# Output rounds of a two-product kernel: spread evenly over the steps and started three steps earlier, with another start and tail

## The chip, the cores and the metric

The kernel runs on one core of a Trainium2 chip. The metric is the device time of one execution in microseconds (us). The granted clock is the share of TensorE's full clock that the profile lists; half clock is 0.5. Ratios are the mean time of one kernel's runs over that of the other's runs of the same rounds on the same chip, so they are not quite the ratio of the medians that stand beside them.

## The reference, cut to what matters

```python
# a 7-tap causal convolution along the sequence, taps by softmax, one set per head
w = softmax(weight)                                   # 8 heads x 7 taps
att = einsum('hk,bskhg->bshg', w, windows(x))         # 8 x 4096 x 192
# then two products with ELU between
h = att.reshape(32768, 192) @ w_in                    # 192 x 2048
g = where(h > 0, h, exp(min(h, 0)) - 1)
out = g @ w_out                                       # 2048 x 192, float32
```

## The kernel before

The tokens go through in 32 tiles of 1024, each in 16 steps of 128 hidden columns. I write h(n) for the first product of step n. Steps are counted from 0, over the whole run (h(16) opens tile 1) or, in the listings, within a tile (h(4) is the one of its step 4). ACT is ScalarE, POOL GpSimd and DVE VectorE; PSUM is the memory that TensorE writes its products to, and SBUF the memory that holds the operands. One step is this chain over four engines:

```python
# TensorE: h(n), six matmuls into slot k of three PSUM slots (two banks each)
wait_slot(k)                 # the step (or convolution) that had this slot is through with it
for j in range(3):
    for r in range(2):       # two row tiles of 64, one bank each
        matmul(H[:, k % 3, GS*r : GS*(r+1)], w_in[...], att[...], start=(j == 0), ...)
# ACT, then POOL, then DVE, two halves of 512 columns each
E  = exp(H)                                  # ACT
E  = max(min(E, 1), 0)                       # POOL
gT = max(E - 1, H)                           # DVE; frees the slot
```

The second product is made of output rounds. A round is two matmuls, one per row tile of 64, into the two banks of the accumulator `ops`. A half (256 of 512 token rows in each of two groups) takes 64 rounds: every piece of gT is used with row tile 0 into bank 0 and row tile 1 into bank 1, and once more with the banks exchanged. Two row tiles may not add into one bank at the same time, so TensorE waits at an exchange for the run of rounds before it. The Trainium skill (PSUM — Partial Sum Buffer, "PSUM bank collisions raise a hardware error") has it that different row tiles cannot access one bank at once and that software must order them.

```python
LAG = -1                                     # first output round of tile t: step 16(t+1)-1
HALF_STEPS = (10, 10, 6, 6, 10, 11, 11)      # rounds in 7 of 8 steps; none in the eighth
CONV_AT = ((4, 1, 1), (12, 2, 0))            # a convolution in steps 4 and 12 of a tile
...
            mid = (r0 + r1) // 2 if convs else r1
            order.append(("o", t, half, r0, mid))
            for k, g in convs:
                conv_at(k, g)                # in the middle of its step's rounds
            if mid < r1:
                order.append(("o", t, half, mid, r1))
...
                    for r in range(r0, r1):
                        second, (q, kb) = r // (NR // 2), divmod(r % (NR // 2), 2)
                        W(s_tt, 2 * (NQ * t + q) + 2)            # gT is there
                        if second:
                            W(s_swap, 2 * (2 * t + half + 1))    # one exchange a half
```

A convolution takes one of the three PSUM slots as well, and ACT copies it out (1.02 us). At the end of each half ACT copies the accumulator out (`osb`, 0.82 us); the first round of the next half waits for that copy.

## Time and profile before

| | before |
|---|---|
| time, median (before the change was run) | 756.66 us |
| span of the profiled run | 754.1 us |
| eight steps (half a tile) with a convolution | 11.32 us |
| first product of tile 1 starts (step 16) | 38.3 us |
| start of the last first product to the end | 16.6 us |

The page's busy times, with the share of the span and the number of instructions of each engine (PEld is TensorE's weight load):

```profile
PE 739.3 (98%) x13860; PEld 512.0 (68%) x13860; DVE 635.7 (84%) x1041; ACT 646.8 (86%) x1163; POOL 660.2 (88%) x1104
```

The groups of instructions with most time (line, engine, what is written and read; busy time, mean ns of one; idle time ahead of them and who ended it):

```profile
L500 DVE SCALAR_TENSOR_TENSOR gT<-E,H 128x512 f16<-128x512 f32 x1024 | 630.5, 681 | 98.7 <-POOL E L354 90.4
L437 ACT ACTIVATE E<-H 128x512 f32<-128x512 f32 x1024 | 546.2, 605 | 86.9 <-PE H L646 73.4
L676 PE MATMUL ops<-w_out,gT 64*128 64x192 f16 x8064 | 414.6, 243 | 0.9 <-DVE gT L500 0.9
L646 PE MATMUL H<-att,w_in 64*128 64x512 bf16 x3072 | 409.5, 379 | 5.7 <-DMA w_in<-w_in 3.4
```

TensorE hardly waits for anybody; DVE, ACT and POOL have 99, 87 and 79 us of idle time ahead of these instructions (POOL's line is not shown). The mean times of one matmul (243 and 379 ns) are from its start to its modelled end and overlap, so the pace is read from starts. Here is the order of time of TensorE over the steps around a convolution (start, us to the modelled end of the last one, what, how many):

```profile
404.78 0.66 PE L676 MATMUL ops<-w_out,gT 64*128 64x192 f16 x12
405.32 0.82 PE L646 MATMUL H<-att,w_in 64*128 64x512 bf16 x6
405.98 0.99 PE L676 MATMUL ops<-w_out,gT 64*128 64x192 f16 x20
406.80 0.81 PE L646 MATMUL H<-att,w_in 64*128 64x512 bf16 x6
407.45 0.57 PE L676 MATMUL ops<-w_out,gT 64*128 64x192 f16 x10
407.96 0.66 PE L619 MATMUL H<-Tr,xg 128*24 128x24 bf16 x40
408.55 0.67 PE L676 MATMUL ops<-w_out,gT 64*128 64x192 f16 x12
409.06 0.81 PE L646 MATMUL H<-att,w_in 64*128 64x512 bf16 x6
409.70 1.07 PE L676 MATMUL ops<-w_out,gT 64*128 64x192 f16 x22
410.61 1.46 PE L646 MATMUL H<-att,w_in 64*128 64x512 bf16 x12
```

From 405.32 to 405.98 six matmuls of a first product are issued (0.65 us); from 405.98 to 406.80 ten rounds (0.082 us each). Everything stands shoulder to shoulder. The step with the convolution is the one that starts at 406.80, which I call h(4). From h(4) to h(6) at 410.61 are 3.81 us. The last line holds two first products at once (x12): the step without rounds. ACT in the same stretch:

```profile
407.66 1.09 ACT L437 ACTIVATE E<-H 128x512 f32<-128x512 f32 x2 [0.39 <-PE H L646]
408.67 1.02 ACT L417 ACTIVATE csb<-H 128x1024 bf16<-128x1024 f32 x1
409.91 1.09 ACT L437 ACTIVATE E<-H 128x512 f32<-128x512 f32 x2 [0.21 <-PE H L646]
410.88 0.82 ACT L408 ACTIVATE osb<-ops 128x768 f32<-128x768 f32 x1
411.57 0.62 ACT L437 ACTIVATE E<-H 128x512 f32<-128x512 f32 x1
```

The matmuls of h(6) end at 411.42 or so (410.61 + 0.81); its Exp starts at 411.57, 0.11 us later than ACT could, because of the copy-out of the accumulator. In square brackets stands the idle time of the engine and who ended it.

Last, the stretches of the run by windows (us of each engine's busy time, granted clock, DMA share, GB/s): to h(16), to h(32), to the last first product, to the end.

```profile
12.00:38.30 26.30, 19.08 (x218) 7.51 (x216) 18.96 (x31) 18.97 (x37) 18.29 (x31) 0.87 0.71 128
38.30:61.70 23.40, 23.33 (x472) 16.38 (x474) 18.90 (x31) 20.21 (x36) 19.27 (x33) 1.00 0.40 86
61.70:737.50 675.80, 675.80 (x12820) 472.07 (x12816) 589.27 (x958) 599.29 (x1075) 611.70 (x1023) 1.00 0.43 95
737.50:754.10 16.60, 11.98 (x264) 10.58 (x260) 4.33 (x7) 3.73 (x7) 2.90 (x5) 1.00 0.24 73
```

In the 675.8 us of the third line TensorE is busy for 675.8. The first line holds the only slow clock (mean 0.87): at the start TensorE waited 3.4 us for a part of w_in that is copied inside SBUF, and ran at half clock from 16.9 to 23.7 us.

### The profile page before, as it was taken

What the parts mean: (1) busy time and instruction counts of PE and PEld (TensorE: products, weight loads), DVE (VectorE), ACT (ScalarE), POOL (GpSimd) and SP (SyncE); (2) the same over time, 40 slices, a digit from 0 to 9 for tenths busy, and PEclk for the clock granted to TensorE, in tenths of its full rate; (3) what the DMA queues carried; (4) which work ended last, traced back from release to release, by engine and by line L of the source; (5) the groups of instructions that cost most, each with busy time, mean ns of one, the idle gap of its engine ahead of it and who ended that gap; (6) DMA issues with size and microseconds to landing.
All of it is one profiled execution on the core that took longest, in us unless ns stands there. A gap on an engine that the chain in (4) does not pass through costs nothing.

```text
span 754.1 us, 32225 instructions
## 1 busy us (share of the span) xinstructions
PE 739.3 (98%) x13860; PEld 512.0 (68%) x13860; DVE 635.7 (84%) x1041; ACT 646.8 (86%) x1163; POOL 660.2 (88%) x1104
## 2 busy tenths in 40 slices
PE   6899999999999999999999999999999999999997
PEld 3367667767767767767767767767767767767676
DVE  3888898888888888888888888888888888888893
ACT  3888888888888888888888888889889889889882
POOL 5888998998998998998998998998998998998882
PEclk9899999999999999999999999999999999999999
DMA  9434345354355354355354355354355354355112
GB/s 176 101 87 93 93 105 112 77 107 92 92 108 110 76 109 91 93 108 110 75 111 92 89 110 109 74 112 92 88 112 109 72 114 90 87 115 107 58 44 64
DMA packets 106590, 72.79 MB, mean 97 GB/s; under 512 B 44488, under 2 KB 105808, under 8 KB 106448
## 3 DMA queue, kind: packets, MB, share of 16 engines
q1 hardware_dynamic: 66432, 54.77, 24.1%
q0 software_dynamic: 39600, 15.39, 19.1%
q8 instruction: 108, 1.77, 1.0%
q10 hardware_dynamic: 416, 0.59, 0.3%
q14 instruction: 34, 0.28, 0.1%
HBM read 44.00 MB, written 41.42 MB: 113 GB/s over the span
## 4 chain that ended last, share of the span: by engine, by line
PE 94%; DMA 2%; ACT 1%; DVE 1%; issue 0%; POOL 0%; SPq 0%
PE H L646 45%; PE ops L676 44%; PE H L619 5%; DMA w_in<-w_in 1%; DMA w_in<-in_moe_w_in_dram 1%; PE H L676 1%; ACT E L437 1%; DVE gT L500 1%; DMA att<-conv_slots 0%; DMA conv_slots<-csb 0%; ACT csb L417 0%; PE ops L537 0%; POOL w_in L312 0%; POOL E L354 0%; SPq L279 0%
## 5 line engine op out<-in xcount | busy, mean ns | idle before, releaser
L500 DVE SCALAR_TENSOR_TENSOR gT<-E,H 128x512 f16<-128x512 f32 x1024 | 630.5, 681 | 98.7 <-POOL E L354 90.4
L354 POOL TENSOR_SCALAR E<-E 128x512 f32<-128x512 f32 x1024 | 605.5, 615 | 78.7 <-ACT E L437 76.3
L437 ACT ACTIVATE E<-H 128x512 f32<-128x512 f32 x1024 | 546.2, 605 | 86.9 <-PE H L646 73.4
L676 PEld LDWEIGHTS ops<-w_out,gT 64*128 64x128 f16 x8064 | 342.2, 94 | 109.7 <-ACT osb L408 10.8
L676 PE MATMUL ops<-w_out,gT 64*128 64x192 f16 x8064 | 414.6, 243 | 0.9 <-DVE gT L500 0.9
L646 PE MATMUL H<-att,w_in 64*128 64x512 bf16 x3072 | 409.5, 379 | 5.7 <-DMA w_in<-w_in 3.4
L646 PEld LDWEIGHTS H<-att,w_in 64*128 64x128 bf16 x3072 | 130.5, 94 | 107.6 <-DVE gT L500 4.2
L417 ACT ACTIVATE csb<-H 128x1024 bf16<-128x1024 f32 x60 | 61.4, 1024 | 0.0
L408 ACT ACTIVATE osb<-ops 128x768 f32<-128x768 f32 x63 | 51.5, 817 | 5.1 <-PE ops L676 5.1
L307 POOL DMA_DIRECT2D xg<-in_x_dram x62 | 52.2, 842 | 0.4 <-issue 0.4
L619 PE MATMUL H<-Tr,xg 128*24 128x122 bf16 (+1 forms) x2400 | 39.3, 209 | 0.0
L619 PEld LDWEIGHTS H<-Tr,xg 128*24 128x24 bf16 x2400 | 30.1, 92 | 9.5 <-issue 9.5
L511 DVE COPY osb<-H 128x384 f32<-128x384 f32 x1 | 0.6, 558 | 8.9 <-PE H L676 8.9
L537 PE MATMUL ops<-zw 64*128 64x512 bf16 x20 | 4.6, 455 | 1.6 <-ACT csb L417 1.6
L532 PE MATMUL ops<-zw 128*128 128x512 bf16 x11 | 4.9, 632 | 1.3 <-DVE zw L450 1.3
L676 PE MATMUL H<-w_out,gT 64*128 64x192 f16 x128 | 5.6, 243 | 0.1
L676 PEld LDWEIGHTS H<-w_out,gT 64*128 64x128 f16 x128 | 5.2, 94 | 0.3 <-PE H L676 0.3
L400 ACT ACTIVATE osb<-H 128x384 f32<-128x384 f32 x1 | 0.5, 491 | 4.7 <-PE H L676 4.7
L532 PEld LDWEIGHTS ops<-zw 128*128 128x128 bf16 x11 | 1.5, 144 | 3.7 <-issue 2.5
L537 PEld LDWEIGHTS ops<-zw 64*128 64x128 bf16 x20 | 1.2, 110 | 4.0 <-ACT csb L417 2.6
L375 ACT ACTIVATE xT<-H 64x24 bf16<-64x24 f32 x1 | 0.2, 188 | 3.4 <-PE H L556 3.4
L312 POOL DMA_DIRECT2D w_in<-in_moe_w_in_dram x4 | 2.7, 680 | 0.3 <-DMA wh<-in_weight_dram 0.3
(46 smaller groups left out, 27.8 us busy)
## 6 DMA issues: line engine op xcount, KB each, us to landing
out_dram<-osb SPq DMA_DIRECT2D x127, 192.0 KB, 2.7
conv_slots<-csb SPq DMA_DIRECT2D x62, 256.0 KB, 2.5
att<-conv_slots SPq DMA_DIRECT2D x186, 64.0 KB
xg<-in_x_dram POOLq DMA_DIRECT2D x31, 240.0 KB, 5.0
xg<-in_x_dram POOLq DMA_DIRECT2D x31, 192.0 KB, 4.4
w_out<-in_moe_w_out_dram POOLq DMA_DIRECT2D x1, 768.0 KB, 16.2
xf<-in_x_dram ACTq DMA_DIRECT2D x1, 384.0 KB, 3.1
xf<-in_x_dram SPq DMA_DIRECT2D x1, 384.0 KB, 3.7
```

The source lines that it names most:

```text
L307: g.dma_start(xg[:, b, w0:w1, :], src).then_inc(s_x[b][part - 1], 16)
L312: g.dma_start(w_in[HP * r : HP * (r + 1), :, c0:c1], moe_w_in.rearrange("(p j) f -> p j f", j=3)[:, :, c0:c1],).then_inc(s_w[k], 16)
L354: g.tensor_scalar(out=E[:, n % NE, u, :], in0=E[:, n % NE, u, :], scalar1=1.0, scalar2=0.0, op0=ALU.min, op1=ALU.max,).then_inc(s_clp)
L408: a.activation(osb[:, b, :, :, :].rearrange("p g k d -> p g (k d)"), ops[:, :, 0 : 2 * D], ACT.Copy,).then_inc(s_oev)
L417: return a.activation(csb[:, m % 4, b0:b1, :], conv_bank(m)[:, b0:b1, :], ACT.Copy)
L437: a.activation(E[:, n % NE, u, :], H[:, k, GS * u : GS * (u + 1)], ACT.Exp).then_inc(s_exp)
L500: v.scalar_tensor_tensor(out=gT[:, s % NG3, q, u, :], in0=E[:, n % NE, u, :], scalar=1.0, in1=H[:, slot_of_pair[n] % 3, GS * u : GS * (u + ...
L532: pe.matmul(ops[:, 0, :], zw[:, 0:P], zw[:], start=True, stop=True)
L537: pe.matmul(ops[:, r, :], zw[HP * r : HP * (r + 1), 0:P], zw[HP * r : HP * (r + 1), :], start=True, stop=True, tile_position=(HP * r, 0),)
L619: ins = pe.matmul(to[SLOT * q : SLOT * q + CPH, hb, o : o + nc_], xg[:, s % NXB, w, CPH * h : CPH * (h + 1)], Tr[:, h, CW - c0 - nc_ : CW ...
L646: ins = pe.matmul(H[:, k % 3, GS * r : GS * (r + 1)], w_in[HP * r : HP * (r + 1), j, FC * q : FC * (q + 1)], att[HP * r : HP * (r + 1), s ...
L676: ins = pe.matmul(acc[:, g, D * kb : D * (kb + 1)], gT[HP * rt : HP * (rt + 1), t % NG3, q, g, t0 : t0 + P], w_out[HP * rt : HP * (rt + 1) ...
```

## The change

The change has four parts: output rounds start at step 12 of their tile instead of step 15, so that fewer are left for the tail; each step has eight rounds, and row tiles and banks are exchanged at each step, so that a round needs only the gT pieces that are already there; the rounds of the tail are interleaved so that they need not wait for an exchange; and the start loads w_in in four chunks, three of them straight to both halves of SBUF, and casts x first. The core of the diff:

```diff
-LAG = -1
-WCOLS = ((0, 256), (256, 1024), (1024, 2048))
-Q_PART = (0,) * 2 + (1,) * 6 + (2,) * 8
-WARM = (11, 1)
-HALF_STEPS = (10, 10, 6, 6, 10, 11, 11)
+LAG = -4
+QB = 4
+WCOLS = ((0, 256), (256, 640), (640, 1280), (1280, 2048))
+Q_PART = (0,) * 2 + (1,) * 3 + (2,) * 5 + (3,) * 6
+WARM = (9, 1)
...
+            for i in range(2 * NQ // QB):
+                n = NQ * (t + 1) + LAG + 8 * half + i
+                q0 = QB * (i // 2)
+                rounds_at[n] = [
+                    (t, half, q, kb, i % 2) for q in range(q0, q0 + QB) for kb in range(2)
+                ]
...
+    tail = (
+        piece(0, 0, 8, 14, (0, 1)) + piece(1, 0, 0, 12, (0,))
+        + piece(0, 1, 8, 14, (0, 1)) + piece(1, 1, 0, 12, (0,))
+        + piece(1, 0, 0, NQ, (1,))
+        + piece(0, 1, 14, NQ, (0, 1)) + piece(1, 1, 12, NQ, (0,))
+        + piece(0, 0, 14, NQ, (0, 1)) + piece(1, 0, 12, NQ, (0,))
+        + piece(1, 1, 0, NQ, (1,))
+    )
...
+        slot_of_pair[n] = take_slot(("h", n))
+        order.append(("h", n))
+        if n in EARLY_CONV:
+            conv_at(*EARLY_CONV[n])
         if s:
-            convs += [(s + ahead, g) for at, ahead, g in CONV_AT if at == i and n < NP]
+            for at, ahead, g in CONV_AT:
+                if at == i and s + ahead < NS:
+                    conv_at(s + ahead, g)
         if n in rounds_at:
-            mid = (r0 + r1) // 2 if convs else r1
-            order.append(("o", t, half, r0, mid))
-            for k, g in convs:
-                conv_at(k, g)
-            if mid < r1:
-                order.append(("o", t, half, mid, r1))
+            order.append(("o", rounds_at[n]))
...
             load_w_in(0, (0, 1))
-            load_w_in(1, (0,))
-            for part in (1, 2):
-                load_x(1, part)
-            load_w_in(2, (0,))
+            load_w_in(1, (0, 1))
+            load_x(1, 1)
+            load_w_in(2, (0, 1))
+            load_x(1, 2)
+            load_w_in(3, (0,))
```

The convolution now stands right behind h(4), ahead of all rounds of its step. And a half now ends in the step before that one, without a step free of rounds behind it.

The recorded texts say swap for exchange, evacuation for copy-out, product for first product, and twelfth step for step 12.

More of the change, by code (lines that the diff above doesn't have):

```diff
@@ L68, in bass_lightweight_conv__then__act_elu_kernel @@
     NQ = FF // FC
-    NR = 4 * NQ
     assert NQ == 16
@@ L76, in bass_lightweight_conv__then__act_elu_kernel @@
     x_flat = x.rearrange("b s d -> (b s) d")
-    steps = []
     slot_of_pair, slot_of_conv, prior = {}, {}, []
@@ L89, in bass_lightweight_conv__then__act_elu_kernel @@
     order = []
-    last_half = (NS - 1, 1)
-    last_slot = None
     def conv_at(s, g):
@@ L97, in conv_at @@
         order.append(("c", m))
+    last = NS - 1
     rounds_at = {}
     for t in range(NS):
-        base = NQ * (t + 1) + LAG
         for half in range(2):
-            r = 0
-            for i, cnt in enumerate(HALF_STEPS):
-                rounds_at[base + 8 * half + i] = (t, half, r, r + cnt)
-                r += cnt
-            assert r == NR
-    for n in range(NP + NQ + LAG):
+            for i in range(2 * NQ // QB):
[4 more added lines that the diff above has]
+                ]
@@ new lines, in piece @@
+    def piece(half, turned, q0, q1, kbs):
+        return [(last, half, q, kb, turned) for q in range(q0, q1) for kb in kbs]
+    tail = (
[6 more added lines that the diff above has]
+    )
+    rounds_at = {n: rounds for n, rounds in rounds_at.items() if n < NP}
@@ L109, in bass_lightweight_conv__then__act_elu_kernel @@
+    for n in range(NP):
         s, i = divmod(n, NQ)
-        if n < NP:
-            slot_of_pair[n] = take_slot(("h", n))
-            order.append(("h", n))
-        convs = [EARLY_CONV[n]] if n in EARLY_CONV else []
+        slot_of_pair[n] = take_slot(("h", n))
+        order.append(("h", n))
+        if n in EARLY_CONV:
+            conv_at(*EARLY_CONV[n])
         if s:
-            convs += [(s + ahead, g) for at, ahead, g in CONV_AT if at == i and n < NP]
-        convs = [(k, g) for k, g in convs if k < NS]
+            for at, ahead, g in CONV_AT:
+                if at == i and s + ahead < NS:
+                    conv_at(s + ahead, g)
@@ L117, in bass_lightweight_conv__then__act_elu_kernel @@
         if n in rounds_at:
-            t, half, r0, r1 = rounds_at[n]
-            if (t, half) == last_half and r0 == 0:
-                last_slot = take_slot(None)
-            mid = (r0 + r1) // 2 if convs else r1
-            order.append(("o", t, half, r0, mid))
-            for k, g in convs:
-                conv_at(k, g)
-            if mid < r1:
-                order.append(("o", t, half, mid, r1))
-        else:
-            for k, g in convs:
-                conv_at(k, g)
+            order.append(("o", rounds_at[n]))
@@ new lines, in bass_lightweight_conv__then__act_elu_kernel, with acc_of @@
+    last_slot = [take_slot(None) for _ in range(2)]
+    order.append(("o", tail))
+    def acc_of(t, half, kb):
+        return (t, half, kb if (t, half) == (last, 1) else 0)
+    total, done = {}, {}
+    for item in order:
+        if item[0] == "o":
+            for t, half, q, kb, turned in item[1]:
+                key = acc_of(t, half, kb)
+                total[key] = total.get(key, 0) + 1
+    runs, stops = [], {}
+    last_run = {}
+    for x_, item in enumerate(order):
+        if item[0] != "o":
+            continue
+        ends = []
+        for y, (t, half, q, kb, turned) in enumerate(item[1]):
+            key = acc_of(t, half, kb)
+            if not runs or runs[-1][0] != (key, turned, x_):
+                runs.append([(key, turned, x_), (x_, y), (x_, y), last_run.get(key)])
+                last_run[key] = len(runs) - 1
+            runs[-1][2] = (x_, y)
+            done[key] = done.get(key, 0) + 1
+            if done[key] == total[key]:
+                ends.append(key)
+                stops[x_, y] = key
+        item += (ends,)
+        order[x_] = item
@@ L132, in bass_lightweight_conv__then__act_elu_kernel @@
+    run_from = {run[1]: (k, run[3]) for k, run in enumerate(runs)}
+    run_to = {run[2] for run in runs}
+    mm2_done = {key: 2 * (k + 1) for key, k in last_run.items()}
+    finished = [key for item in order if item[0] == "o" for key in item[2]]
+    place = {key: k for k, key in enumerate(finished)}
     taps = nc.dram_tensor("conv_taps", (HEADS, ZW), BF16).ap()
@@ L171, in bass_lightweight_conv__then__act_elu_kernel @@
         ops = psum("ops", [P, 2, GS])
-        s_w = [sema(f"s_w{i}") for i in range(4)]
+        s_w = [sema(f"s_w{i}") for i in range(5)]
         s_wd = sema("s_wd")
@@ L179, in bass_lightweight_conv__then__act_elu_kernel @@
         s_wb = sema("s_wb")
-        s_wc = [sema(f"s_wc{i}") for i in range(2)]
+        s_wc = sema("s_wc")
         s_id = sema("s_id")
@@ L206, in bass_lightweight_conv__then__act_elu_kernel @@
         s_att = [sema(f"s_att{i}") for i in range(2)]
-        s_mm2 = sema("s_mm2")
         s_swap = sema("s_swap")
@@ L255, in conv_read, with out_group @@
             W(s_ce, m + 1)
-        def out_group(eng, t, half, g):
+        def out_group(eng, t, half, g, kb=None):
             b = (2 * t + half) % 2
             row = SUP * t + GS * g + 2 * P * half
+            if kb is not None:
+                eng.dma_start(
+                    out[row + P * kb : row + P * (kb + 1), :], osb[:, b, g, kb, :]
+                ).then_inc(s_out[b], 16)
+                return
             dst = out[row : row + 2 * P, :].rearrange("(k p) d -> p k d", p=P)
@@ L344, in _gpsimd @@
                 w_out[:, :, :], moe_w_out.rearrange("(q p) d -> p q d", p=FC)
-            ).then_inc(s_w[3], 16)
+            ).then_inc(s_w[4], 16)
             load_x(2, 2)
@@ L393, in _scalar, with evac @@
             ).then_inc(s_ha)
-            def evac(t, half):
+            def evac(key):
+                t, half, kb = key
                 n_half = 2 * t + half
-                W(s_mm2, n_half + 1)
+                W(s_swap, mm2_done[key])
                 b = n_half % 2
                 W(s_out[b], 32 * (n_half // 2))
-                if (t, half) == last_half:
-                    a.activation(
-                        osb[:, b, 0, :, :].rearrange("p k d -> p (k d)"),
-                        H[:, last_slot % 3, 0 : 2 * D],
-                        ACT.Copy,
-                    ).then_inc(s_oev)
-                    W(s_od, 1)
-                    out_group(a, t, half, 1)
+                if (t, half) == (last, 1):
+                    if kb == 0:
+                        a.activation(
+                            osb[:, b, :, 0, :],
+                            H[:, last_slot[0] % 3, :].rearrange("p (g t) -> p g t", g=2)[:, :, 0:D],
+                            ACT.Copy,
+                        ).then_inc(s_oev)
+                    else:
+                        a.activation(
+                            osb[:, b, 0, 1, :], H[:, last_slot[1] % 3, 0:D], ACT.Copy
+                        ).then_inc(s_oev)
+                        W(s_od, 1)
+                        out_group(a, t, half, 1, 1)
                     return
@@ L442, in _scalar @@
                 else:
-                    _, t, half, r0, r1 = item
-                    if r1 == NR:
-                        evac(t, half)
+                    for key in item[2]:
+                        evac(key)
         @block.vector
@@ L473, in _vector @@
             ).then_inc(s_wp)
+            W(s_xl[1], 16)
+            v.tensor_copy(xh[:, 1, :, :], xf[:, 1, :, :]).then_inc(s_xh)
             W(s_wb, 1)
@@ L480, in _vector @@
             ).then_inc(s_D)
-            W(s_xl[1], 16)
-            v.tensor_copy(xh[:, 1, :, :], xf[:, 1, :, :]).then_inc(s_xh)
             W(s_tp, 3)
@@ L496, in _vector @@
                 if s >= NG3:
-                    W(s_mm2, 2 * (s - NG3 + 1))
+                    W(s_swap, mm2_done[s - NG3, 1, 0])
                 for u in range(2):
@@ L508, in _vector @@
             b = (2 * NS - 1) % 2
-            W(s_mm2, 2 * NS)
+            W(s_swap, mm2_done[last, 1, 1])
             W(s_out[b], 32 * (NS - 1))
             v.tensor_copy(
-                osb[:, b, 1, :, :].rearrange("p k d -> p (k d)"),
-                H[:, last_slot % 3, GS : GS + 2 * D],
+                osb[:, b, 1, 1, :], H[:, last_slot[1] % 3, GS : GS + D]
             ).then_inc(s_od)
@@ L600, in _tensor @@
                 ins.then_inc(s_hc)
-            for item in order:
+            for x_, item in enumerate(order):
                 if item[0] == "c":
@@ L633, in _tensor @@
                         W(s_hd, 2)
-                    elif n < NQ - 1 and not any(n - 2 <= e < n for e in EARLY_CONV):
+                    elif n < NQ + LAG and not any(n - 2 <= e < n for e in EARLY_CONV):
                         conv_read(W, sum(e < n for e in EARLY_CONV) - 1)
                         warm_pair(WARM[1])
-                    if Q_PART[q]:
-                        W(s_wc[Q_PART[q] - 1], 16)
+                    if Q_PART[q] < 3:
+                        W(s_w[Q_PART[q]], 32)
                     else:
-                        W(s_w[0], 32)
+                        W(s_wc, 16)
                     W(s_att[s % 2], 16 * NDMA_ATT * ((s + 1) // 2))
@@ L655, in _tensor @@
                 else:
-                    _, t, half, r0, r1 = item
-                    W(s_w[3], 16)
-                    if (t, half) == last_half:
-                        acc = H[:, last_slot % 3, :].rearrange("p (g t) -> p g t", g=2)
-                        if r0 == 0:
-                            wait_slot(last_slot)
-                    else:
-                        acc = ops
-                        if r0 == 0:
-                            conv_read(W, FREE_CONV - 1)
-                            W(s_oev, 2 * t + half)
@@ L667, in _tensor @@
-                    for r in range(r0, r1):
-                        second, (q, kb) = r // (NR // 2), divmod(r % (NR // 2), 2)
-                        W(s_tt, 2 * (NQ * t + q) + 2)
-                        if second:
-                            W(s_swap, 2 * (2 * t + half + 1))
+                    W(s_w[4], 16)
+                    for y, (t, half, q, kb, turned) in enumerate(item[1]):
+                        key = acc_of(t, half, kb)
+                        W(s_tt, 2 * (NQ * t + q) + 2)
+                        begins = False
+                        if (x_, y) in run_from:
+                            k, prev = run_from[x_, y]
+                            begins = prev is None
+                            if prev is not None:
+                                if runs[prev][0][1] != turned:
+                                    W(s_swap, 2 * (prev + 1))
+                            elif (t, half) == (last, 1):
+                                wait_slot(last_slot[kb])
+                            else:
+                                conv_read(W, FREE_CONV - 1)
+                                W(s_oev, place[key])
+                        if (t, half) == (last, 1):
+                            acc = H[:, last_slot[kb] % 3, :].rearrange("p (g t) -> p g t", g=2)
+                            d0 = 0
+                        else:
+                            acc, d0 = ops, D * kb
+                        ends = (x_, y) in stops
@@ L673, in _tensor @@
                         t0 = 2 * P * half + P * kb
                         for rt in range(2):
-                            g = rt ^ second
+                            g = rt ^ turned
                             ins = pe.matmul(
-                                acc[:, g, D * kb : D * (kb + 1)],
+                                acc[:, g, d0 : d0 + D],
                                 gT[HP * rt : HP * (rt + 1), t % NG3, q, g, t0 : t0 + P],
                                 w_out[HP * rt : HP * (rt + 1), q, :],
-                                start=(r == 0),
-                                stop=(r == NR - 1),
+                                start=begins,
+                                stop=ends,
@@ L682, in _tensor @@
                                 tile_position=(HP * rt, 0),
                             )
-                            if r == NR // 2 - 1:
+                            if (x_, y) in run_to:
                                 ins.then_inc(s_swap)
-                    if r1 == NR:
-                        ins.then_inc(s_mm2)
         @block.sync
@@ L700, in _sync @@
             ).then_inc(s_band, 16)
-            for k in (1, 2):
-                c0, c1 = WCOLS[k]
-                W(s_w[k], 16)
-                sy.dma_start(
-                    w_in[HP:P, :, c0:c1], w_in[0:HP, :, c0:c1]
-                ).then_inc(s_wc[k - 1], 16)
+            c0, c1 = WCOLS[3]
+            W(s_w[3], 16)
+            sy.dma_start(w_in[HP:P, :, c0:c1], w_in[0:HP, :, c0:c1]).then_inc(s_wc, 16)
             for item in order:
@@ L725, in _sync @@
                 elif item[0] == "o":
-                    _, t, half, r0, r1 = item
-                    if r1 < NR:
-                        continue
-                    W(s_oev, 2 * t + half + 1)
-                    for g in range(1 if (t, half) == last_half else 2):
-                        out_group(sy, t, half, g)
+                    for key in item[2]:
+                        t, half, kb = key
+                        W(s_oev, place[key] + 1)
+                        if (t, half) != (last, 1):
+                            for g in range(2):
+                                out_group(sy, t, half, g)
+                        elif kb == 0:
+                            for g in range(2):
+                                out_group(sy, t, half, g, 0)
+                        else:
+                            out_group(sy, t, half, 0, 1)
             for b in range(2):
-                sy.wait_ge(s_out[b], 32 * NS)
+                sy.wait_ge(s_out[b], 32 * NS + 32 * b)
 _INS = ['x', 'weight', 'moe_w_in', 'moe_w_out']
```

## The prediction

> **What bounds it now.** TensorE. The page has PE at 98%; the windows view has it 100% busy from 60 to 735 us at full clock. The order of time shows each step's first product (six matmuls) issuing in 0.65 us and an output round (two matmuls) in 0.082 us, back to back. One half-tile of eight steps costs 8 x 0.65 + 64 x 0.082 + one convolution (0.69, switching included) = 11.15 us; measured: 11.32. The remaining 0.17 us are three short waits for a DVE release in the steps of ten and six rounds. Besides: a start-up wait for w_in (TensorE idle 14.5 to 17.9 us, then half clock to 23.7) and a tail of 16.6 us from the start of the last product.
>
> **What the change gives.**
> - Start: two direct w_in chunks replace the copied one that caused the wait, and x is cast about 1.8 us earlier. The next limits are the copied last chunk and the chain convolution, bounce, att (8.5 us from product 10 to product 16). I expect product 16 some 4 us earlier (38.3 now).
> - Tail: 22 fewer output rounds and no evacuation wait: about -3.7 us.
> - Even rounds remove the 0.17 us waits.
>
> **What it costs.** The first product reuses a PSUM slot after ACT, POOL and DVE finished with it: 2.72 us after the product's last matmul ends, 3.53 after its start. A convolution takes a slot too, so around it slots return after two products. Before, 22 rounds lie between; h(4) to h(6) took 3.81 us of issue against 3.53. After, the convolution stands at once behind h(4), and only 16 rounds lie between. Also the half now ends the step before, so the 0.82 us evacuation of the accumulator sits on ACT ahead of the Exp of h(4) (ACT reissues 0.69 us after it), and delays that Exp by 0.36 us (0.11 now).
>
> My walk of one half, with the trace's durations: the convolution waits 0.27 us for its slot; the evacuation itself hides behind the convolution; h(5) waits 0.05, h(6) 0.36. Half: 8 x 1.308 + 0.59 + 0.68 = 11.74 us, +0.42 for 59 halves = +25 us. Three halves without a convolution wait 0.6 us more each for the evacuation: +2. All of it is critical: TensorE is the bound.
>
> Swapping row tiles and banks waits for the previous run; a first product lies between, so this is free. The Trainium skill (TensorEngine Tiling (Array Packing), Key Properties) says that a change of tiling mode drains TensorE; the trace agrees: 0.172 us before the convolution against 0.080 between rounds. The half clock after the start-up wait agrees with TensorE: Matmul & The Clock Gate, Part 1.
>
> **Predicted:** 757 + 27 - 4 - 4 = 776; shaded for a better steady state: 773 us, 748 to 787. Faster by over 2%: 0.08; within: 0.37; slower: 0.55.
>
> **What would show it.** Right: sixteen steps take about 23.5 us in the order of time (22.65 before); first product and convolution waiting for DVE gT in the waits view, near 0.3 us each, twice per sixteen steps; PE below 97% in the middle slices; product 16 near 34 us; last product to end about 13 us. Wrong: sixteen steps at 22.3 us with no such waits.
>
> **What would make it wrong.** A shorter chain Exp, min, subtract-max than 2.72 us; a start that gains 8 us or, if the last w_in chunk is late, nothing.

## The result

The changed kernel takes 776.45 us (median of 4, 776.25 to 778.58) against 756.14 us (median of 4) before: ratio 1.0275, 95% interval 1.0246 to 1.0304. It is slower. The profiled run is the one of 778.58 us, span 776.8.

The page of the changed kernel:

```profile
PE 742.2 (96%) x13852; PEld 517.9 (67%) x13852; DVE 660.5 (85%) x1041; ACT 649.3 (84%) x1164; POOL 665.9 (86%) x1107
```

The same four stretches by windows (h(16) now starts at 35.6 us, h(32) at 61.5):

```profile
12.00:35.60 23.60, 17.47 (x254) 8.41 (x254) 19.68 (x32) 18.48 (x36) 18.84 (x32) 1.00 0.84 141
35.60:61.50 25.90, 25.15 (x473) 17.57 (x474) 18.44 (x29) 20.47 (x36) 19.32 (x32) 0.93 0.41 86
61.50:763.60 702.10, 680.04 (x12822) 477.28 (x12820) 613.84 (x959) 602.02 (x1076) 615.27 (x1022) 1.00 0.42 92
763.60:776.80 13.20, 9.57 (x220) 8.76 (x214) 3.78 (x7) 3.25 (x7) 2.49 (x5) 1.00 0.19 61
```

The ends of the stretches give the ledger of the two profiled runs:

| stretch | before | after | difference |
|---|---|---|---|
| to h(16) | 38.3 | 35.6 | -2.7 |
| h(16) to h(32) | 23.4 | 25.9 | +2.5 |
| h(32) to the last first product | 675.8 | 702.1 | +26.3 |
| last first product to the end | 16.6 | 13.2 | -3.4 |

So the middle lost 26.3 us, the tail won 3.4, and the start won 2.7. Of the 2.5 us lost up to h(32), some 0.85 are the loss of the middle again (two halves); the other 1.6 I put down to the half clock after the start (see below). Now the order of time of TensorE in the middle; h(4) starts at 407.49:

```profile
406.18 0.81 PE L689 MATMUL H<-att,w_in 64*128 64x512 bf16 x6
406.83 0.82 PE L724 MATMUL ops<-w_out,gT 64*128 64x192 f16 x16
407.49 0.81 PE L689 MATMUL H<-att,w_in 64*128 64x512 bf16 x6
408.49 0.65 PE L662 MATMUL H<-Tr,xg 128*24 128x122 bf16 x40 [0.18 <-DVE gT L544]
409.06 0.83 PE L724 MATMUL ops<-w_out,gT 64*128 64x192 f16 x16
409.74 0.81 PE L689 MATMUL H<-att,w_in 64*128 64x512 bf16 x6
410.38 0.82 PE L724 MATMUL ops<-w_out,gT 64*128 64x192 f16 x16
411.38 0.82 PE L689 MATMUL H<-att,w_in 64*128 64x512 bf16 x6 [0.18 <-DVE gT L544]
```

There are two holes. The issue of h(4) is over at 408.14, and the convolution starts at 408.49: 0.35 us, of which some 0.09 are the change of tiling that was there before too. The rounds of h(5) are over at 411.04 (410.38 + 8 x 0.082), and h(6) starts at 411.38: 0.34 us. The brackets show only 0.18 of each, because the modelled ends of the matmuls reach into the holes. From h(4) to h(6) are 3.89 us; before they were 3.81, with 22 rounds inside instead of 16. Both holes end with a release by DVE, the last engine that uses a slot. ACT there:

```profile
408.01 0.82 ACT L453 ACTIVATE osb<-ops 128x768 f32<-128x768 f32 x1
408.70 1.11 ACT L482 ACTIVATE E<-H 128x512 f32<-128x512 f32 x2
409.65 1.07 ACT L462 ACTIVATE csb<-H 128x1024 bf16<-128x1024 f32 x1
```

The matmuls of h(4) end at 408.30, so its Exp could start at 408.34 (0.04 us later, as elsewhere); it starts at 408.70, behind the copy-out of the accumulator: 0.36 us late. Everything behind it is late by as much, down to the slot that h(6) needs. In the waits of the 640 us from 60 to 700 us (engine, who it waited for: us, times, longest) TensorE stands with two lines that the kernel before does not have at all:

```profile
PE H L662 <- DVE gT L544: 10.2, 54, 0.2
PE H L689 <- DVE gT L544: 8.2, 48, 0.2
```

Eight steps now take 11.75 us.

### The profile page after: what moved, and what is told of

It is laid out like the page before. It is cut to its first block, busy times and chain, and to the rows that moved or that the text cites. A ratio compares the mean times of both kernels' runs of the same rounds, so it can differ in the third digit from the quotient of the medians.

```text
span 776.8 us, 32216 instructions
## 1 busy us (share of the span) xinstructions
PE 742.2 (96%) x13852; PEld 517.9 (67%) x13852; DVE 660.5 (85%) x1041; ACT 649.3 (84%) x1164; POOL 665.9 (86%) x1107
## 3 DMA queue, kind: packets, MB, share of 16 engines
q1 hardware_dynamic: 66384, 54.47, 23.5%
## 4 chain that ended last, share of the span: by engine, by line
PE 62%; DVE 11%; ACT 10%; issue 10%; POOL 5%; DMA 2%; SPq 0%
PE H L689 33%; PE ops L724 27%; DVE gT L544 11%; ACT E L482 7%; POOL E L393 5%; ACT osb L453 3%; DMA conv_slots<-csb 1%; PE H L724 1%; DMA att<-conv_slots 1%; DMA xf<-in_x_dram 0%; SPq L317 0%; PE H L631 0%; PE ops L631 0%; PE H L611 0%; PE H L599 0%
## 5 line engine op out<-in xcount | busy, mean ns | idle before, releaser
L544 DVE SCALAR_TENSOR_TENSOR gT<-E,H 128x512 f16<-128x512 f32 x1024 | 655.4, 684 | 99.8 <-POOL E L393 91.3
L482 ACT ACTIVATE E<-H 128x512 f32<-128x512 f32 x1024 | 558.0, 601 | 111.0 <-PE H L689 110.8
L689 PE MATMUL H<-att,w_in 64*128 64x512 bf16 x3072 | 416.7, 377 | 15.8 <-DVE gT L544 11.0
L689 PEld LDWEIGHTS H<-att,w_in 64*128 64x128 bf16 x3072 | 135.8, 94 | 95.6 <-DVE gT L544 27.9
L462 ACT ACTIVATE csb<-H 128x1024 bf16<-128x1024 f32 x60 | 64.3, 1071 | 0.0
L350 POOL DMA_DIRECT2D w_in<-in_moe_w_in_dram x7 | 4.6, 657 | 0.3 <-DMA wh<-in_weight_dram 0.3
L580 PE MATMUL ops<-zw 64*128 64x512 bf16 x14 | 2.7, 377 | 0.8 <-ACT csb L462 0.8
L462 ACT ACTIVATE csb<-ops 128x512 bf16<-128x512 f32 x4 | 2.6, 638 | 0.0
```

What stands on the lines that cost most here:

```text
L350: g.dma_start(w_in[HP * r : HP * (r + 1), :, c0:c1], moe_w_in.rearrange("(p j) f -> p j f", j=3)[:, :, c0:c1],).then_inc(s_w[k], 16)
L462: return a.activation(csb[:, m % 4, b0:b1, :], conv_bank(m)[:, b0:b1, :], ACT.Copy)
L482: a.activation(E[:, n % NE, u, :], H[:, k, GS * u : GS * (u + 1)], ACT.Exp).then_inc(s_exp)
L544: v.scalar_tensor_tensor(out=gT[:, s % NG3, q, u, :], in0=E[:, n % NE, u, :], scalar=1.0, in1=H[:, slot_of_pair[n] % 3, GS * u : GS * (u + ...
L580: pe.matmul(ops[:, r, :], zw[HP * r : HP * (r + 1), 0:P], zw[HP * r : HP * (r + 1), :], start=True, stop=True, tile_position=(HP * r, 0),)
L689: ins = pe.matmul(H[:, k % 3, GS * r : GS * (r + 1)], w_in[HP * r : HP * (r + 1), j, FC * q : FC * (q + 1)], att[HP * r : HP * (r + 1), s ...
```

## The experiments

Theory A is the one of the prediction: slots come back too late around the convolution, since only 16 rounds stand where 22 stood, and the copy-out of the accumulator now sits on ACT ahead of the Exp of h(4). Rival B: each exchange of row tiles and banks costs a drain, and there are seven a half in place of one. A third reading is that even rounds, or rounds from step 12 on, are bad by themselves. In each kernel "eight steps" is read from the starts of the first products.

### 1. The exchanges alone

The kernel before, its rounds only reordered so that it exchanges at each step:

```diff
-    second, (q, kb) = r // (NR // 2), divmod(r % (NR // 2), 2)
+    second, q, kb = table[r]     # table: (exchanged, from, to) in pieces of gT:
+    # (0, 0, 10), (1, 0, 10), (0, 10, 16), (1, 10, 16), (0, 16, 26), (1, 16, 32), (0, 26, 32)
```

(cut: the waits and signals at each exchange, which follow the table)

> The kernel before with its own round counts (10, 10, 6, 6, 10, 11, 11, none), but row tiles and banks swapped at each step, seven times a half instead of once. Theory A (slots come back too late around the convolution, the evacuation delays an Exp; swaps are free because a first product lies between): eight steps stay at 11.3 to 11.45 us (one of the swaps now falls inside a step and may cost 0.1), the whole 755 to 763 us. Rival B (each swap costs TensorE a drain, and seven of them are the 0.43 us that the change added to a half): eight steps near 11.7 us, the whole near 778 us.

Measured: 768.93 us (ratio 1.0198, 1.0181 to 1.0215), eight steps 11.51. That is neither: more than A said, less than B. The timeline tells where. The step in which two runs meet with nothing between is this line:

```profile
402.12 1.34 PE L683 MATMUL ops<-w_out,gT 64*128 64x192 f16 x22
```

These 11 rounds take 1.17 us to the next start at 403.30, against 0.91 before (409.70 to 410.61): one exchange inside a step costs 0.27 us, where I had guessed 0.1. (Eight steps are only 0.19 longer: the rest came out of short waits that the kernel before had, 0.88 us for its second step of ten rounds against 0.83 here.) The other exchanges, between steps, show nothing: ten rounds take 0.825 us. But as the experiment mixed both, it did not decide; experiment 9 is its repetition.

### 2. The copy-out taken away

The changed kernel; from the second tile on ACT copies only 4 of 384 columns of each bank (a wrong result; every wait stays):

```diff
+    width = 2 * D if n_half < 2 else 4
-    ops[:, :, 0 : 2 * D],
+    ops[:, :, 0:width],
```

> The changed kernel, but from the second tile on the evacuation of the accumulator reads only 4 of 384 columns of each bank (wrong result on purpose). Theory A: the Exp behind it starts 0.36 us earlier, and with it the slot of that product comes back; what is left is the slot wait around the convolution: eight steps 11.38 us instead of 11.75, the whole 753 to 758 us. Rival B (swaps) and rival D (only start and tail moved): eight steps stay at 11.75, the whole at 776.

Measured: 755.02 us, eight steps 11.41 (11.38 expected), ratio to before 1.001. There are as many exchanges, and 0.34 of the 0.43 us are gone. TensorE's wait for the slot of h(6) is gone from the waits, and the one of the convolution stays, as A has it:

```profile
PE H L663 <- DVE gT L545: 10.5, 56, 0.2
```

Rival B falls as an account of most of the loss.

### 3. Even rounds in the kernel before

```diff
-HALF_STEPS = (10, 10, 6, 6, 10, 11, 11)
+HALF_STEPS = (8, 8, 8, 8, 8, 8, 8, 8)
```

> The kernel before with eight rounds in each step in place of 10, 10, 6, 6, 10, 11, 11 and none; nothing else. Theory A: now the first round of a half waits 0.77 us for the evacuation (no convolution stands there to cover it), and the product two behind the convolution 0.2 us for its slot: eight steps 12.1 us, the whole 800 to 808 us. If even rounds by themselves were harmless: 11.15 to 11.3 us, 748 to 756 us.

Measured in a single run (state unknown): 805.16 us, eight steps 12.13. Here nothing stands between the end of a half and the next one's first round but one first product, and TensorE waits for ACT:

```profile
PE ops L676 <- ACT osb L408: 30.6, 53, 0.6
PEld H L646 <- DVE gT L500: 14.4, 52, 0.3
```

So the odd row of numbers in the kernel before, with its step of no rounds, was worth 0.8 us in eight steps. In the changed kernel the convolution takes the place of that step: it covers the copy-out.

### 4. The convolution behind the rounds

The changed kernel, with the lines that place the convolution moved behind the one that places the rounds.

> The changed kernel with the convolution behind the eight rounds of its step instead of ahead of them. Theory A: the slot waits of the convolution and of the product two behind it go (more issue lies between), but the first round now waits about 0.76 us for the evacuation, which the convolution covered: eight steps 11.9 us, the whole about 786 us; TensorE then waits for ACT osb and no longer for DVE gT. If the evacuation were no matter, only the slots: 11.1 to 11.2 us, 740 to 745 us.

Measured in a single run (state unknown): 787.47 us, eight steps 11.90. TensorE now waits for the copy-out and not for DVE:

```profile
PE ops L724 <- ACT osb L453: 31.2, 54, 0.6
```

The wait only changes its name. Ahead of the rounds the convolution hides the copy-out but asks for its slot too early; behind them the reverse.

### 5 and 8. Uneven rounds in the changed kernel

```diff
-QB = 4                         # 8 rounds in each step
+PAIRS = (11, 6, 6, 9)          # run 5: 11, 11, 6, 6, 6, 6, 9, 9 rounds
+PAIRS = (10, 7, 7, 8)          # run 8: 10, 10, 7, 7, 7, 7, 8, 8
```

(cut: the lines that deal the rounds out, and the list of the tail's rounds, which is fitted to them)

> The changed kernel with uneven rounds in place of eight per step: counted from the convolution's step, 11, 11, 6, 6, 6, 6, 9, 9; start, tail, swaps and the place of the convolution stay as changed. Theory A: 22 rounds again lie between the product in the convolution's step and the one two behind it, whose slot comes back 5.20 us into my walk, just when TensorE gets there; the nine rounds ahead of the boundary cover the convolution's own slot. One short wait of 0.1 us is left: eight steps 11.27 us, the whole 746 to 752 us, faster than both kernels. Rival B (each swap costs): stays near 11.7 us, about 775 us, since there are as many swaps.

> The changed kernel with rounds 10, 10, 7, 7, 7, 7, 8, 8. Theory A: the slot wait of the convolution (0.27 us) stays, since the eight rounds ahead of it stay; the one of the product two behind it falls to 0.08 us: eight steps 11.40 us, the whole 754 to 757 us. So of two distributions that both have fewer rounds in the middle, only the one with more rounds ahead of the convolution as well gets to 11.27.

Measured: run 5 759.76 us (ratio to before 1.0064, 1.0044 to 1.0084), eight steps 11.44 to 11.46, one half in eight 11.53; run 8 758.82 us (1.0048), eight steps 11.42, one half in eight 11.51. Both get most of the 0.43 us back with the same exchanges, start and tail. But the first was to reach 11.27 and to beat both kernels, and does not; the second is near its 11.40, yet 1.8 us above its range of 754 to 757. In its timeline the wait of the convolution is still there (from the start of h(4) to that of the convolution 0.89 us; it is 0.995 in the changed kernel, and would be some 0.74 with no wait: 0.65 of issue and 0.09 for the change of tiling). DVE tells why:

```profile
405.84 7.40 DVE L550 SCALAR_TENSOR_TENSOR gT<-E,H 128x512 f16<-128x512 f32 x12 [0.26 <-POOL E L399]
```

DVE works twelve instructions off without a gap, one per 0.6 us, 1.2 us a step. A step of six rounds takes TensorE only 1.14 us (0.65 + 6 x 0.082), so over four of them DVE falls behind, and the slots come back at DVE's pace and not at the 2.72 us of an empty chain. My walk took the empty chain everywhere. This is read from the trace; no run was spent on it.

### 6. The first convolutions earlier

Run 5's kernel with `EARLY_CONV = {4: (1, 0), 7: (1, 1), 16: (2, 0)}` in place of `{5: ..., 9: ..., 16: ...}`.

> The kernel of the run ahead of this one with the first two convolutions at products 4 and 7 instead of 5 and 9. If the start is bound by the chain convolution, bounce, att into product 16, that product begins 2 us earlier (35.6 us in the changed kernel, 33 to 34 here) and the whole is 2 us shorter. If the transfers that still load (w_out, x) bind the chain, product 16 moves by less than 0.5 us.

Measured: 759.78 us, the same as run 5 (759.76), though in the profiled runs h(16) starts at 34.1 us instead of 36.0. (Run 8 has the start of run 5 and h(16) at 34.6, so much of this is what differs from run to run.) The single runs of each kernel spread over 758.2 to 762.7 us. Five of the six with a mean clock of 1.000 took 758.2 to 758.8 us (the sixth 760.0); the six with 0.996 to 0.998 took 759.6 to 762.7. A gain of 2 us is thus not shown, and what binds the start stays open.

### 7. The start alone

The kernel before with the start of the changed one (w_in chunks, cast, nine warm-up matmuls).

> The kernel before with the start of the changed one alone (four w_in chunks, three of them loaded directly to both halves, x cast first, nine warm-up matmuls). Product 16 near 35.6 us as in the changed kernel instead of 38.3; the whole 752 to 754 us, if no half clock follows the wait for att, and 755 if it does. Eight steps stay at 11.32 us.

Measured: 752.61 us (ratio 0.9965, 0.9951 to 0.9979), eight steps 11.32, h(16) at 34.2. The start by itself is good for 2.7 us of the median.

### 9. The exchanges alone, without the flaw

As experiment 1, with the last two entries of the table cut at the convolution: `(1, 16, 21), (0, 26, 32), (1, 21, 32)`. Seven exchanges a half, a first product or a convolution between any two runs.

> The first experiment again without its flaw: the kernel before with seven swaps a half, six between steps (a first product lies between) and one where the convolution stands inside a step, none with two output rounds side by side. If only a swap with nothing between costs (0.27 us, as that run's timeline shows): eight steps 11.32 us as before, the whole 753 to 757 us plus about 1 us in the tail, where nothing lies between. If swaps cost in general: 11.5 us or more, 767 us.

Measured: 757.62 us (ratio 1.0039), eight steps 11.31 to 11.33 as before. The 3 us are in the tail, where about 1 was expected: 18.8 us from the last first product against 16.6, and 0.26 us more in each of the last two halves, where no convolution stands between. The step with the convolution:

```profile
407.78 0.58 PE L683 MATMUL ops<-w_out,gT 64*128 64x192 f16 x10
408.29 0.66 PE L626 MATMUL H<-Tr,xg 128*24 128x24 bf16 x40
408.88 0.67 PE L683 MATMUL ops<-w_out,gT 64*128 64x192 f16 x12
```

Apart from the tail this is the kernel before to a hundredth of a microsecond. In its tail the gap between two rounds at an exchange is 0.33 us where it is 0.08 otherwise. An exchange costs 0.25 to 0.27 us with nothing between, and in these steps nothing otherwise. Rival B is refuted.

### 10 and 11. A combination

The changed kernel (start, tail, rounds from the twelfth step, exchanges) with the row of rounds of before, and with the convolutions moved by three steps, so that they stand among the rounds where they stood before:

```diff
-QB = 4
+HALF_STEPS = ((0, 0, 10),), ((1, 0, 10),), ((0, 10, 16),), ((1, 10, 16),), ((0, 16, 26),), \
+    ((1, 16, 21), (0, 26, 32)), ((1, 21, 32),)    # the convolution between the two parts
-CONV_AT = ((4, 1, 1), (12, 2, 0))
-EARLY_CONV = {5: (1, 0), 9: (1, 1), 16: (2, 0)}
-X_AT = ((5, 1), (10, 0), (13, 2))
+CONV_AT = ((1, 1, 1), (9, 2, 0))
+EARLY_CONV = {5: (1, 0), 9: (1, 1), 13: (2, 0)}   # run 11: 16
+X_AT = ((2, 1), (7, 0), (10, 2))
```

> The changed kernel's start, tail and early output rounds (from the twelfth step) with the round counts of before (10, 10, 6, 6, 10, 5 + 6 around the convolution, 11, none) and the convolutions moved by three steps so that they stay where they stood among the rounds. Theory A: eight steps 11.32 us, tail 13.2 us from the last product instead of 16.6, product 32 near 58 us: the whole 747 to 750 us, faster than both kernels by 1% against before and 3.6% against the changed one. If the early output rounds themselves (twelfth step on) cost anything, eight steps are longer than 11.35.

> The same with the third early convolution left at product 16 (13 in the run ahead). It then stands one step ahead of the next one, so slots are short there once: 0 to 1 us longer than the run ahead, eight steps in the middle equal.

Measured: run 10 751.84 us (ratio to before 0.9960, 0.9944 to 0.9975), run 11 752.49 us (0.9974, 0.9955 to 0.9993). Both are correct and faster than both kernels (both intervals lie below 1), but less than expected: eight steps are 11.33 and 11.40 in turn. That run 11 takes 0.65 us more is within the spread of the runs. The copy-out is whole here, and the exchanges and the early rounds are kept: what undid the loss is where the convolution stands and how the rounds are dealt out. The long half has its time in one place. These are the steps of six rounds of run 10, first in the short, then in the long half:

```profile
409.30 0.82 PE L692 MATMUL H<-att,w_in 64*128 64x512 bf16 x6
409.96 0.66 PE L727 MATMUL ops<-w_out,gT 64*128 64x192 f16 x12
410.50 0.82 PE L692 MATMUL H<-att,w_in 64*128 64x512 bf16 x6
```

```profile
420.61 0.82 PE L692 MATMUL H<-att,w_in 64*128 64x512 bf16 x6
421.27 0.66 PE L727 MATMUL ops<-w_out,gT 64*128 64x192 f16 x12
421.89 0.82 PE L692 MATMUL H<-att,w_in 64*128 64x512 bf16 x6
```

The rounds take 0.54 us to the next first product in the one and 0.62 in the other. The second is the first product of a new tile, h(16s), which has one more wait: for att, although att landed many steps ago. The waits give this to nobody (28 waits ended by "issue", one per tile).

### 12. The wait for att moved

```diff
                     W(s_att[s % 2], 16 * NDMA_ATT * ((s + 1) // 2))
+                    if q == 13 and s and s + 1 < NS:
+                        W(s_att[(s + 1) % 2], 16 * NDMA_ATT * ((s + 2) // 2))
```

> The combined kernel (third early convolution at 13) has one half of each pair 0.07 us longer than before (11.40 against 11.33): its timeline shows the time just ahead of the first product of a tile, which waits for att besides its slot, though att landed long ago, and the profile puts it to issue. Here TensorE waits for att at product 13 of the tile ahead, where nothing else is waited for. If the second wait at that place is the cause: both halves 11.33 us, the whole 1.5 to 2 us less than the combined kernel, 749.5 to 751 us. If not (a slot that comes back late there): no change, 751.8 us.

Measured: 748.58 us (748.07 to 749.66), ratio to before 0.9914 (0.9896 to 0.9932): 0.9% faster than the kernel before, correct. Both halves are at 11.31 to 11.33, as expected; the time is a little below the expected 749.5 to 751. The same place as above, in this run:

```profile
418.62 0.66 PE L729 MATMUL ops<-w_out,gT 64*128 64x192 f16 x12
419.16 0.82 PE L694 MATMUL H<-att,w_in 64*128 64x512 bf16 x6
```

In run 10 h(16s) starts 0.146 us after the end of DVE's work on the slot that it takes, in this run 0.057 us, in every tile of the middle; the first product of the other half behind six rounds, h(16s+8), has 0.057 in both. So TensorE did wait for the slot there, and the second wait held it for 0.09 us more. In the kernel before, the slot is free 0.20 us ahead of h(16s), and its step takes no longer than others of ten rounds: there the same two waits cost nothing.

The middle is 2.6 us shorter than in run 10 (676.8 for 679.4), where 1.5 to 2 were expected of the whole; the rest of the gain is in the start of the profiled runs (h(32) at 56.9 for 58.2 us), which differs from run to run by as much.

## Why the prediction was right, point by point

- **The bound.** Right. TensorE issues before with no gap but some 0.17 us of short waits a half, and each hole that opened in the changed kernel is in the time.
- **The walk through one half.** Right to a hundredth: 11.74 us predicted, 11.75 measured. The terms: the convolution waits 0.27 (0.35 with the change of tiling), h(6) 0.36 (0.34), the Exp of h(4) is 0.36 us late (0.36). Experiment 2 takes the copy-out away and finds 11.41 where the walk has 11.38; experiments 3 and 4 find 12.13 and 11.90 for 12.1 and 11.9.
- **The middle.** +27 was predicted for 62 halves from h(12) on; the 60 or so of them between h(32) and the last first product took +26.3: 0.43 for a half with a convolution, and 0.58 for each of the two whole halves without one, where 0.6 was predicted.
- **The exchanges are free.** Right where a product or a convolution lies between (experiment 9). My later guess of 0.1 us for one with nothing between was wrong: 0.27 (experiment 1).
- **A change of tiling mode drains TensorE** (the Trainium skill, TensorEngine Tiling (Array Packing), Key Properties): the trace of the kernel before agrees, with 0.172 us ahead of the convolution against 0.080 between rounds, some 0.09 more. In the changed kernel this cannot be told apart from the wait for the slot.
- **The tail.** -3.7 predicted, -3.4 measured.
- **The start.** This term was mis-sized: "product 16 some 4 us earlier" was 2.7 in the profiled run, and the start alone was worth 2.7 us in experiment 7. Up to h(32) the profiled run then lost 2.5 us: 0.85 are what two halves lose anywhere (23.50 us for 22.65), and the other 1.6 I put down to the clock, with no run made for it. TensorE, idle from 32.5 to 35.6 us in the wait for att, ran at half clock from 37.0 to 40.5 us, within the stretch of mean clock 0.93. That idle time is followed by half clock is what the Trainium skill says (TensorE: Matmul & The Clock Gate, Part 1), and I had named it only for the kernel before. The page asks for at least one idle window of about 3.4 us; here 3.2 us of idle time went ahead, in run 8 2.5 us, while 2.8 us in run 11 were not followed by half clock, so the length of the idle time alone does not tell. The three other runs of the changed kernel list a clock of 1.000 and took 776.25 to 776.53, 2.1 to 2.3 us less than the profiled one.
- **The shading.** The sum of the terms was 776; I put 773 "for a better steady state". There was no reason in the trace for that, and the measured 776.45 is the unshaded sum. That sum came out a little well: the start gave less than thought, and the profiled runs are 22.7 us apart where the medians are 20.3.
- **What would show it.** Sixteen steps took 23.50 (23.5 said); the waits for DVE are there twice per sixteen steps, each hole 0.34 to 0.35 us wide in starts but listed as 0.18; the middle stretch has TensorE busy 680.0 of 702.1 us, 96.9%.

What stays open is what binds the start (experiment 6), and how much of the wait in run 5 belongs to DVE's pace alone.

## What to carry to other kernels

In a pipeline over few buffers, count the issue time between the claim of a buffer and the next claim of the same one, at the tightest place (here: around the convolution, which takes a slot out of turn), and hold it against the chain that gives the buffer back, other work on those engines included; an even spread of work can be worse than an odd one that was fitted to that place. Where a copy-out sits in its engine's order decides what it delays, so place a release that can be covered behind work that covers it. And take an early, easily met wait away from the spot where the engine already waits for something else: it was worth 0.09 us a tile here, and the middle became 2.6 us shorter.

## What the Trainium skill lacked or had wrong

- TensorEngine Tiling (Array Packing), Gotcha 1, tells that row tiles may not use one bank at once and that software must order them, but not what ordering costs: an exchange of row tiles and banks between two runs of rounds cost 0.25 to 0.27 us with nothing between, and nothing behind a first product of 0.65 us or a convolution (experiments 1 and 9).
- The same page, Key Properties, gives no figure for the drain at a change of tiling mode: between rounds and convolution TensorE took about 0.09 us more than between rounds (0.172 between starts, against 0.080); that this is the drain is not shown apart.
- Perfetto Trace Analysis, Identifying Dependency Chains, tells that an instruction with several waits may have extra wait instructions ahead of it, but that section does not tell what such a wait can cost: on TensorE, for a semaphore that had long been raised, beside a wait that was still open, about 0.09 us once per tile (0.146 us against 0.057 from the release of the slot to the start, experiments 10 and 12).
